# Clustered attention and a rational MLP on one core: a new order of the operations on all five engines

## The chip, the cores and the metric

The kernel runs on one core of one Trainium2 chip. The metric is the device time of one execution in microseconds (us); the time of a kernel is the median of its runs. The trace is that of one profiled execution. Engines are named as in the profile: PE (TensorE), DVE (VectorE), ACT (ScalarE), POOL (GpSimd) and SP (SyncE, which here only issues transfers).

## The reference

Attention in which a query attends to the keys of its own cluster alone, and behind it an MLP whose activation is a quotient of two polynomials:

```python
q_assign = np.argmax(np.einsum('bhsd,hcd->bhsc', q_n, c_n), axis=-1)
k_assign = np.argmax(np.einsum('bhsd,hcd->bhsc', k_n, c_n), axis=-1)
mask = q_assign[:, :, :, None] == k_assign[:, :, None, :]
scores = np.where(mask, scale * np.matmul(q, k.transpose(0, 1, 3, 2)), -1e9)
attn = np.exp(scores - scores.max(-1, keepdims=True))
attn = attn / (attn.sum(-1, keepdims=True) + 1e-9)
x = np.matmul(attn, v).transpose(0, 2, 1, 3).reshape(B * S, H * D)
h = x @ w_in
g = (a[0] + a[1]*h + a[2]*h**2 + a[3]*h**3) / (1 + abs(b[0])*abs(h) + abs(b[1])*h**2 + 1e-6)
out = g @ w_out
```

Here q_n, k_n and c_n are the normalised rows. B = 4, H = 8, S = 768, D = 64, 16 clusters, w_in is 512 x 2048 and w_out 2048 x 512, all in float32.

## The kernel before

Every operand of a matrix product is split into a high and a low float16 half, so that a product is three matmuls. The work goes batch by batch. For each of four pairs of heads `prep` (L944) loads q and k, scales and splits them into `tk` and `tq` (the high half is copied a second time at L1092, and each of the two buffers is transposed by a DMA at L1120), finds the clusters (L1159 to L1208) and splits v into `vhi` and `vlo` (L1249). `attend` (L1256) takes two tiles of 128 queries at a time: scores on PE (`s`, L1278), the maximum on DVE (L1293), the exponential and the high half on ACT (all of ACT's activations stand at the helper's line L551), the low half on DVE (`ah`, L1313), a transpose by DMA (`at<-ah`, L1323), the product with v on PE (`px`, L1332; four groups of 18 matmuls make one `px` bank), the division on DVE (`inv`, `xf`, L1352 to L1358), the split of the result (`xm`, on ACT and on POOL at L1365) and its transpose `x` by DMA (L1372). Batch 0 mostly uses another form, `attend_keys` (L1378). `moe` (L1582) takes 256 tokens and four blocks of 128 columns at a time: `ph` on PE (L1640), |h| and the first step of the cubic on ACT (`u`, `t`), two more steps of it on DVE (`t`, L1661 and L1666, which free the PSUM bank of `ph`), the denominator on POOL (`s`, L1680, L1686, L1703) and ACT, the quotient on DVE (`t`, `s`, L1723, L1733), its low half on POOL (`u`, L1740), and the second product on PE (`po`, L1751), whose sum goes out through `ob`.

A `px` bank and the two `ph` banks come from the same small ring of PSUM banks, so a `px` can start only when the DVE has finished the two `t` operations on an earlier `ph`.

What sets the order: the functions above run no instruction themselves. They hand operations to `Plan` (`op`, L212), with the buffers that each reads and writes, and `Plan.order` (L260) decides in which order they are emitted. It holds the table `ORDER`, five lists, one for each engine, of running numbers of operations. With the table given, each engine takes its operations strictly in the list's order:

```python
turn_of = {e: [self.ops[i] for i in reversed(self.given[e])] for e in engines}
```

An operation still waits, by semaphores, for what it reads and for the buffer that it writes. Within that, `Plan.order` runs a model of the engines that decides in which sequence the five lists are interleaved, and from it which slot of a ring of buffers (eight large buffers, five `ah`, three `at`, two `rv`, two PSUM banks for `ph` and `px`, two for `s`) each tile gets. So a new table moves instructions, the slots of buffers and the places of waits, and nothing else. An engine works strictly in order: an instruction that waits holds up all that stand behind it. The model marks all operations of POOL and some of DVE (`lock=True`: the copies at L1092, the quotient steps at L1723 and L1733) as taking turns at one port.

Of the kernel before, what the change touches and what calls it, by code (L numbers as in the profile page):

```python
# [65 lines left out]
""",  # L66
    "DVE": """
# [103 lines left out]
""",  # L171
}

# [1696 lines left out]
```

## Time and profile before

| what | value |
|---|---|
| three runs | 883.43, 890.54, 881.96 us; median 883.43 us |
| the profiled execution | 889.14 us, its span 887.2 us (1.94 us lie around the span) |
| mean granted PE clock | 0.995 of full speed |
| busy, of the span | PE 94%, DVE 89%, ACT 85%, POOL 65% |
| chain that ended last, by engine | PE 60%, DVE 15%, ACT 11%, DMA 7%, issue 5% |

Busy shares are averages over stages with different limits, so the windows of 40 us and the chain by place say more. The chain is followed back from the last instruction: each piece is what released the next one. On the timelines a bracket at the end of a row gives the engine's idle time just before it and what ended it; POOL's rows often overlap by some hundredths of a microsecond, which means that they ran back to back.

### The profile page before, as it was taken

Reading aid. Unit: us, or ns where it says so; the run is one execution under the profiler, and the core shown is the slowest. Engines: PE = TensorE matmul, PEld = TensorE weight load, DVE = VectorE, ACT = ScalarE, POOL = GpSimd, SP = SyncE. Lnnn points to the kernel's source line nnn. Section 1 sums busy time; section 2 is a strip of 40 time slices with the busy share of each in tenths; the row PEclk is TensorE's granted clock in tenths of the full one; section 3 lists DMA queues with packets and bytes.
Section 4 is the critical chain, followed back from the end, with each engine's and each line's share of the span. In section 5 each row is a group of like instructions: output and inputs, shape, how many; then the busy total and the mean of one; then the engine's idle time right before and its main releaser. Section 6 shows DMA issues by size and latency. Waiting matters only on the chain.

```text
span 887.2 us, 22561 instructions
## 1 busy us (share of the span) xinstructions
PE 835.5 (94%) x8989; PEld 590.7 (67%) x8989; DVE 787.1 (89%) x1396; ACT 757.6 (85%) x1053; POOL 579.0 (65%) x608
## 2 busy tenths in 40 slices
PE   2889998878998999999999999999999999999997
PEld 2557776656676676667676776767677666766763
DVE  6997959999999999999999999999999988767776
ACT  7567799979999899989999999998998888756664
POOL 2264758878777969658778987678767876123221
PEclk9999999999999999999999999999999999999999
DMA  8478688989989699999999999979688887310000
GB/s 289 164 150 197 179 226 212 205 173 160 203 167 207 124 171 199 180 195 211 185 187 165 197 201 165 183 139 186 129 173 138 137 148 116 79 13 24 1 25 24
DMA packets 378025, 138.09 MB, mean 156 GB/s; under 512 B 355776, under 2 KB 372160, under 8 KB 377920
## 3 DMA queue, kind: packets, MB, share of 16 engines
q1 hardware_dynamic: 377920, 136.65, 78.4%
q8 instruction: 70, 1.15, 0.5%
q14 instruction: 35, 0.29, 0.1%
HBM read 41.98 MB, written 6.29 MB: 54 GB/s over the span
## 4 chain that ended last, share of the span: by engine, by line
PE 60%; DVE 15%; ACT 11%; DMA 7%; issue 5%; POOL 1%; SPq 0%; DVEq 0%; ACTq 0%; POOLq 0%
PE ph L1640 19%; PE po L1751 19%; PE px L1332 7%; PE s L1278 7%; DMA at<-ah 4%; ACT s L551 3%; ACT u L551 2%; DVE ah L1313 2%; PE z L1488 2%; DVE s L1293 2%; DMA sq<-tq 2%; DVE top L1436 2%; ACT ah L551 2%; PE px L1507 2%; PE s L1409 1%
## 5 line engine op out<-in xcount | busy, mean ns | idle before, releaser
L1640 PE MATMUL ph<-x,win 128*128 128x256 f16 x2304 | 266.3, 273 | 3.9 <-DVE xf L1358 1.7
L1751 PE MATMUL po<-wout,u 128*128 128x512 f16 x1152 | 268.5, 379 | 0.4 <-DVE u L1740 0.4
L1640 PEld LDWEIGHTS <-win 128*128 128x128 f16 x2304 | 223.9, 98 | 42.9 <-DVE xf L1358 3.5
L1680 POOL TENSOR_TENSOR s<-s,u 128x512 f32<-128x512 f32 x96 | 127.3, 1342 | 119.9 <-ACT s L551 65.3
L1751 PEld LDWEIGHTS <-u 128*128 128x128 f16 x1152 | 110.2, 98 | 115.4 <-DVE u L1740 0.9
L1313 DVE SCALAR_TENSOR_TENSOR ah<-s,ah 128x768 f16<-128x768 f32 x152 | 143.8, 951 | 13.2 <-ACT ah L551 12.6
L551 ACT ACTIVATE s<-s,nm 128x768 f32<-128x768 f32 x152 | 132.4, 874 | 23.1 <-DVE s L1293 18.7
L1293 DVE TENSOR_SCALAR_CACHE_REDUCE s<-s,cc 128x768 f32<-128x768 f32 x144 | 145.2, 1018 | 6.9 <-PE s L1278 6.5
L1278 PE MATMUL s<-sk,sq 128*128 128x384 f16 x608 | 121.1, 326 | 6.6 <-DVE ah L1313 5.4
L551 ACT ACTIVATE ah<-s 128x768 f16<-128x768 f32 x152 | 123.0, 813 | 3.6 <-DMA at<-ah 1.0
L1703 POOL TENSOR_TENSOR s<-s,u 128x512 f32<-128x512 f32 x72 | 111.0, 1553 | 21.3 <-ACT u L551 20.9
L1740 POOL TENSOR_TENSOR u<-s,u 128x512 f16<-128x512 f32 x72 | 85.8, 1200 | 32.1 <-DVE s L1733 17.6
L1332 PEld LDWEIGHTS <-at 128*128 128x128 f16 x2736 | 93.9, 98 | 19.1 <-issue 5.1
L1332 PE MATMUL px<-vhi,at 128*128 128x65 f16 x1824 | 96.7, 195 | 6.2 <-DVE t L1666 3.5
L1332 PE MATMUL px<-vlo,at 128*128 128x64 f16 x912 | 92.5, 193 | 0.0
L1278 PEld LDWEIGHTS <-sq 128*128 128x128 f16 x608 | 55.5, 98 | 45.7 <-DVE ah L1313 8.4
L1661 DVE TENSOR_TENSOR t<-ph,t 128x512 f32<-128x512 f32 x96 | 65.3, 684 | 8.4 <-ACT t L551 8.2
L551 ACT ACTIVATE u<-ph 128x512 f32<-128x512 f32 x96 | 56.8, 596 | 16.5 <-PE ph L1640 16.1
L1733 DVE SCALAR_TENSOR_TENSOR s<-s,t 128x1024 f32<-128x1024 f32 (+1 forms) x49 | 61.5, 1254 | 0.5
L551 ACT ACTIVATE u<-t 128x1024 f16<-128x1024 f32 (+1 forms) x49 | 51.0, 1040 | 11.8 <-DVE t L1723 8.7
L551 ACT ACTIVATE t<-ph,gk 128x512 f32<-128x512 f32 x72 | 55.5, 778 | 0.0
L1723 DVE SCALAR_TENSOR_TENSOR t<-t,gk,u 128x1024 f32<-128x1024 f32 (+1 forms) x37 | 48.4, 1309 | 5.7 <-ACT u L551 5.3
(222 smaller groups left out, 1367.4 us busy)
## 6 DMA issues: line engine op xcount, KB each, us to landing
rwi<-in_moe_w_in_dram SPq DMA_DIRECT2D x16, 512.0 KB, 5.2
rwo<-in_moe_w_out_dram SPq DMA_DIRECT2D x16, 512.0 KB, 5.4
rk<-in_k_dram SPq DMA_DIRECT2D x32, 192.0 KB, 3.0
rq<-in_q_dram SPq DMA_DIRECT2D x32, 192.0 KB, 3.5
rvm<-in_v_dram SPq DMA_DIRECT2D x16, 384.0 KB, 4.6
rv<-in_v_dram SPq DMA_DIRECT2D x16, 384.0 KB, 4.2
out_dram<-ob SPq DMA_DIRECT2D x11, 512.0 KB, 3.8
at<-ah SPq DMA_TRANSPOSE x152, 4.2
```

The source lines that it names most:

```text
L551: lambda: nc.scalar.activation(out=out(), in_=in_(), func=func, **{a: (x() if callable(x) else x) for a, x in kw.items()}),
L1278: nc.tensor.matmul(sc.ap[:, i, :SH], lhsT=st["q" + x].ap[:, j, t, :], rhs=st["k" + x].ap[:, j, ks, :].rearrange("p t c -> p (t c)"), start ...
L1293: lambda nm=nm, view=view: ts(out=view(), in0=view(), scalar1=cc.ap, scalar2=None, op0=ALU.mult, op1=ALU.min, accum_out=nm.ap),
L1313: lambda part=part, view=view: stt(out=part(1), in0=view(), scalar=A_SCALE, in1=part(0), op0=ALU.mult, op1=ALU.subtract),
L1332: nc.tensor.matmul(px.ap[:, i, :w_], lhsT=at.ap[:, p_, kt, :], rhs=vv.ap[:, j, kt, :w_], start=(kt == 0 and vv is vhi and p_ == 0), stop=( ...
L1640: nc.tensor.matmul(ph[i].ap[:, fi * TW : (fi + 1) * TW], lhsT=win[f // 4][:, wpart, c, f % 4 * P : (f % 4 + 1) * P], rhs=xs[c].ap[:, xpart ...
L1661: lambda i=i, th=th, ph=ph: tt(out=th[i].ap, in0=ph[i].ap, in1=th[i].ap, op=ALU.mult),
L1680: lambda i=i, sh=sh, uh=uh: nc.gpsimd.tensor_tensor(out=sh[i].ap, in0=sh[i].ap, in1=uh[i].ap, op=ALU.mult),
L1703: lambda i=i, sh=sh, uh=uh: nc.gpsimd.tensor_tensor(out=sh[i].ap, in0=sh[i].ap, in1=uh[i].ap, op=ALU.mult),
L1733: lambda tw=tw, sw=sw: stt(out=sw(), in0=sw(), scalar=2.0, in1=tw(), op0=ALU.subtract, op1=ALU.mult),
L1740: lambda i=i, sh=sh, gl=gl, g16=g16, e=(nc.vector if gld else nc.gpsimd): e.tensor_tensor(out=gl[i].ap, in0=sh[i].ap, in1=g16()[:, 0, i * ...
L1751: nc.tensor.matmul(po[ti].ap, lhsT=g16()[:, part, c0 : c0 + P], rhs=wout[f // 4][:, wpart, f % 4], start=(k == 0 and f == f_first), stop=( ...
```

## The change

All five lists of `ORDER` are replaced by others. No operation, no buffer, no constant and no line of code is changed. Each list holds the same running numbers as before. Of the operations on PE, 462 of 857 stand at another rank in their list, of those on DVE 751 of 1156, on ACT 591 of 1004, on POOL 455 of 587 and on SP 318 of 394; most by one to five places. One pair of lines of the DVE list as an example (1382 is the copy of keys at L1092, 837 and 838 the two `t` operations at L1661 and L1666, 1265 and 1272 two maxima at L1293):

```diff
-1384 821 1265 817 793 794 795 824 319 320 321 1382 837 838 322 1272 1268 827 828 829 ...
+817 319 793 794 795 824 1265 837 838 320 321 1272 1382 322 1268 827 828 829 ...
```

Three places follow as the engines' instruction streams have them. In a name like `ah_3_5_1_2672` the numbers are the pair of heads, the tile of 128 queries and the head of the pair; in `t_0_0_2699` the block of 256 tokens and the first column block; the last number only tells tiles apart.

First, DVE at about 172 to 178 us of the trace, before:

```order
L1358 TENSOR_TENSOR xf_3_1_2678<-px_3_1_2539,inv_3_1_2669 128x256
L1313 SCALAR_TENSOR_TENSOR ah_3_5_1_2672<-s_3_5_1_2522,ah_3_5_1_2672 128x768
L899 TENSOR_SCALAR g10c_2210<-g10c_2210 128x1
L877 TENSOR_SCALAR g10c_2210<-g10c_2210 128x1
L902 TENSOR_REDUCE g10c_2210<-woe 128x1
L1092 COPY tk_1_2717<-tk_1_2188 128x12x64
L1661 TENSOR_TENSOR t_0_0_2699<-ph_0_0_0_2636,t_0_0_2699 128x512
L1666 SCALAR_TENSOR_TENSOR t_0_0_2699<-t_0_0_2699,gk0c_1244,ph_0_0_0_2636 128x512
L882 TENSOR_TENSOR g10c_2210<-g10c_2210 128x1
L1293 TENSOR_SCALAR s_0_0_1_2725,nm_0_0_1_2755<-s_0_0_1_2725,cc_0_1989 128x2x384
```

And in the changed kernel:

```order
L1358 TENSOR_TENSOR xf_3_1_2672<-px_3_1_2540,inv_3_1_2667 128x256
L1313 SCALAR_TENSOR_TENSOR ah_3_5_1_2669<-s_3_5_1_2581,ah_3_5_1_2669 128x768
L1293 TENSOR_SCALAR s_0_0_0_2525,nm_0_0_0_2692<-s_0_0_0_2525,cc_0_1973 128x2x384
L1661 TENSOR_TENSOR t_0_0_2713<-ph_0_0_0_2634,t_0_0_2713 128x512
L1666 SCALAR_TENSOR_TENSOR t_0_0_2713<-t_0_0_2713,gk0c_1391,ph_0_0_0_2634 128x512
L877 TENSOR_SCALAR g10c_2200<-g10c_2200 128x1
L902 TENSOR_REDUCE g10c_2200<-woe 128x1
L1293 TENSOR_SCALAR s_0_0_1_2720,nm_0_0_1_2754<-s_0_0_1_2720,cc_0_1973 128x2x384
L1092 COPY tk_1_2778<-tk_1_2205 128x12x64
L882 TENSOR_TENSOR g10c_2200<-g10c_2200 128x1
L1313 SCALAR_TENSOR_TENSOR ah_0_0_0_2730<-s_0_0_0_2525,ah_0_0_0_2730 128x768
```

The copy `tk_1` stood ahead of the two `t` operations of the first `ph`; now it stands behind them and behind one more maximum (`s_0_0_1`), and the maximum `s_0_0_0`, which stood ahead of these rows, has come behind `ah_3_5_1`. The small `g10c` operations lie around it in another order.

Second, POOL at about 70 to 77 us, before:

```order
L1194 TENSOR_TENSOR df_2_1025<-df_2_1025,w_90 128x384
L1132 COPY tk_2_719<-mrow 128x12x16
L1133 MEMSET tq_2_975 128x12x16
L1567 TENSOR_TENSOR x_0_0_1099<-rs_0_0_996,x_0_0_1099 128x256
L1208 TENSOR_SCALAR tk_2_719<-df_2_1025 128x12x48
L1208 TENSOR_SCALAR tq_2_975<-df_2_1025 128x12x48
```

And in the changed kernel:

```order
L1132 COPY tk_2_744<-mrow 128x12x16
L1133 MEMSET tq_2_988 128x12x16
L1194 TENSOR_TENSOR df_2_1026<-df_2_1026,w_90 128x384
L1208 TENSOR_SCALAR tk_2_744<-df_2_1026 128x12x48
L1567 TENSOR_TENSOR x_0_0_1098<-rs_0_0_1001,x_0_0_1098 128x256
L1208 TENSOR_SCALAR tq_2_988<-df_2_1026 128x12x48
```

The result of the mask, `tk_2`, is written ahead of `x_0_0` and no longer behind it; `tq_2` stays behind `x_0_0`. SP transposes `tk_2` and then `tq_2`.

Third, DVE at about 453 to 461 us, before:

```order
L1733 SCALAR_TENSOR_TENSOR s_1_0_7139<-s_1_0_7139,t_1_0_7115 128x1024
L1313 SCALAR_TENSOR_TENSOR ah_1_3_0_7321<-s_1_3_0_7255,ah_1_3_0_7321 128x768
L1661 TENSOR_TENSOR t_1_4_7335<-ph_1_4_0_7263,t_1_4_7335 128x512
L1666 SCALAR_TENSOR_TENSOR t_1_4_7335<-t_1_4_7335,gk_3441,ph_1_4_0_7263 128x512
L1293 TENSOR_SCALAR s_1_4_0_7341,nm_1_4_0_7371<-s_1_4_0_7341,cc_1_5819 128x2x384
L1661 TENSOR_TENSOR t_1_4_7335<-ph_1_4_1_7303,t_1_4_7335 128x512
L1666 SCALAR_TENSOR_TENSOR t_1_4_7335<-t_1_4_7335,gk_3441,ph_1_4_1_7303 128x512
L1313 SCALAR_TENSOR_TENSOR ah_1_4_0_7407<-s_1_4_0_7341,ah_1_4_0_7407 128x768
L1293 TENSOR_SCALAR s_1_4_1_7410,nm_1_4_1_7433<-s_1_4_1_7410,cc_1_5819 128x2x384
L1092 COPY tk_3_7437<-tk_3_6772 128x12x64
L1661 TENSOR_TENSOR t_1_8_7431<-ph_1_8_0_7374,t_1_8_7431 128x512
```

And in the changed kernel:

```order
L1733 SCALAR_TENSOR_TENSOR s_1_0_7123<-s_1_0_7123,t_1_0_7103 128x1024
L1661 TENSOR_TENSOR t_1_4_7321<-ph_1_4_0_7264,t_1_4_7321 128x512
L1666 SCALAR_TENSOR_TENSOR t_1_4_7321<-t_1_4_7321,gk_3463,ph_1_4_0_7264 128x512
L1313 SCALAR_TENSOR_TENSOR ah_1_3_0_7337<-s_1_3_0_7255,ah_1_3_0_7337 128x768
L1092 COPY tk_3_7371<-tk_3_6790 128x12x64
L1293 TENSOR_SCALAR s_1_4_0_7345,nm_1_4_0_7376<-s_1_4_0_7345,cc_1_5819 128x2x384
L811 TENSOR_REDUCE vm_7392<-vm_6967 128x1
L1661 TENSOR_TENSOR t_1_4_7321<-ph_1_4_1_7305,t_1_4_7321 128x512
```

The copy `tk_3` has moved up by several places, to directly behind `ah_3_0`. On POOL, what stands around it is the same in both kernels up to the two `xm` at L1365 (two `u`, two `s` of L1680, `s` of L1686, two `xm`); behind these two `xm` the changed list has a `vlo` (L1249), which stood seventeen places later.

Elsewhere on POOL, at about 412 to 416 us, a `vlo` that stood between the two `u` of one block (L1740) now stands five places earlier, ahead of two `s` (L1680), and an `xm` that stood six places later now stands directly ahead of the first of the two `u`. At the end of SP's list one store of the output now stands ahead of the last `x` transpose and no longer behind it.

## Rows read from the trace of the kernel before

**Rows 1.** The page: busy us by engine; POOL at L1680.

```profile
PE 835.5 (94%) x8989; PEld 590.7 (67%) x8989; DVE 787.1 (89%) x1396; ACT 757.6 (85%) x1053; POOL 579.0 (65%) x608
...
L1680 POOL TENSOR_TENSOR s<-s,u 128x512 f32<-128x512 f32 x96 | 127.3, 1342 | 119.9 <-ACT s L551 65.3
```

**Rows 2.** Windows of 40 us: length, busy (instructions), PE clock, DMA share, GB/s.

```profile
160.00:200.00 40.00, 30.01 (x411) 23.88 (x407) 37.88 (x71) 35.28 (x58) 31.47 (x44) 0.96 0.97 180
...
440.00:480.00 40.00, 40.00 (x425) 28.15 (x424) 36.35 (x60) 39.40 (x58) 31.30 (x27) 1.00 0.99 197
```

**Rows 3.** The chain that ended last, 165:186: start, us, what.

```profile
172.25 0.96 DVE ah L1313
...
173.57 3.79 DVE tk L1092
177.36 0.61 DVE t L1661
...
178.89 3.82 PE px L1332 x72
```

**Rows 4.** Timeline of PE, 174 to 180 us.

```profile
174.86 0.81 PE L1278 MATMUL s<-sk,sq 128*128 128x384 f16 x4
178.89 0.22 PE L1332 MATMUL px<-vhi,at 128*128 128x65 f16 x1 [3.22 <-DVE t L1666]
```

**Rows 5.** Timeline of POOL, 172:180: start, us, instruction, idle before.

```profile
173.61 0.68 POOL L1567 TENSOR_TENSOR x<-rs,x 128x256 f16<-128x256 f32 x1
...
177.10 2.62 POOL L1680 TENSOR_TENSOR s<-s,u 128x512 f32<-128x512 f32 x2
179.81 1.05 POOL L1686 TENSOR_SCALAR s<-s 128x1024 f32<-128x1024 f32 x1
```

**Rows 6.** Line L1092: the copies of keys, ns least, median, longest.

```profile
L1092 DVE COPY tk<-tk x12: 348/440/3872, 120.6 to 664.6; 128x768 f16<-128x768 f16 x12
```

**Rows 7.** A window of 2 us in the middle of these `px`.

```profile
180.00:182.00 2.00, 2.00 (x41) 2.00 (x39) 1.54 (x3) 1.20 (x2) 1.99 (x2) 0.50 1.04 318
```

**Rows 8.** The last two `at` transposes: issue in ns, when, landing.

```profile
L1323 SPq DMA_TRANSPOSE at<-ah x2: 1455/1961/2467, 171.7 to 174.2; - x2
...
DMA to landing us min/median/max: 4.0/4.2/4.4
```

**Rows 9.** PE's groups of instructions, 160 to 220.

```profile
L1278 PE MATMUL s<-sk,sq 128*128 128x384 f16 x56 | 11.4, 326 | 4.0 <-DVE ah L1313 4.0
```

**Rows 10.** Timeline of POOL, 66 to 76 us.

```profile
74.24 0.67 POOL L1567 TENSOR_TENSOR x<-rs,x 128x256 f16<-128x256 f32 x1 [3.13 <-ACT x L551]
...
75.53 0.67 POOL L1208 TENSOR_SCALAR tq<-df 128x576 f16<-128x576 f16 x1
```

**Rows 11.** The chain that ended last, 66 to 86 us.

```profile
78.06 5.58 DMA sq<-tq
...
83.69 1.31 PE s L1409 x7
```

**Rows 12.** Timeline of POOL, 405 to 436 us.

```profile
413.13 1.17 POOL L1740 TENSOR_TENSOR u<-s,u 128x512 f16<-128x512 f32 x1
414.25 1.60 POOL L1249 TENSOR_TENSOR vlo<-rv,vhi 128x768 f16<-128x768 f32 x1
```

**Rows 13.** Timeline of PE, 412 to 419 us.

```profile
414.84 1.46 PE L1751 MATMUL po<-wout,u 128*128 128x512 f16 x6
```

**Rows 14.** Timeline of POOL, 452 to 465 us.

```profile
454.17 2.28 POOL L1740 TENSOR_TENSOR u<-s,u 128x512 f16<-128x512 f32 x2 [2.65 <-ACT u L551]
456.91 2.50 POOL L1680 TENSOR_TENSOR s<-s,u 128x512 f32<-128x512 f32 x2 [0.45 <-ACT s L551]
...
460.51 1.30 POOL L1365 TENSOR_TENSOR xm<-xf,xm 128x256 f16<-128x256 f32 x2
463.57 2.32 POOL L1703 TENSOR_TENSOR s<-s,u 128x512 f32<-128x512 f32 x1 [1.76 <-ACT u L551]
```

**Rows 15.** Timeline of DVE, 452 to 465 us.

```profile
455.50 0.75 DVE L1666 SCALAR_TENSOR_TENSOR t<-t,gk,ph 128x512 f32<-128x512 f32 x1
```

258 rows, old and new, of the table ORDER are left out of this document.

## The prediction

> **What bounds the kernel now.** I read the page's busy times first, then the windows of 40 us, then the chain where a window showed idle PE, and last the timelines of what the chain named. PE is the busiest engine, but DVE and ACT are close behind it, so the mean says little [rows 1]. The windows decide: from about 440 us on PE shows 40.00 busy of 40, while DVE has 36.35 and POOL 31.30 [rows 2]. There a better order of DVE, ACT or POOL can give nothing, since PE has no idle time to give back, and a worse one can only add. Between 160 and 200 us it is otherwise: PE is busy for 30.01 of 40, so 10.0 us are idle, and DVE is at 37.88 [rows 2]. That stretch is DVE's, and a gain has to come from there or from ahead of it.
>
> The largest single hole is at 175.7 to 178.9 us. The chain goes through one DVE copy, `tk` at L1092, which holds 3.79 us of it from 173.57 on, then through the `t` operations at L1661 and L1666, and only then `px` begins at 178.89 [rows 3]. PE had finished the scores at 174.86 + 0.81 = 175.67 and then sat idle for 3.22 us, released by that `t` [rows 4]. The copy is a small operation: the median of the twelve is 440 ns, this one took 3872 ns [rows 6]. What stretched it is seen on POOL, which ran back to back from 173.61 to 177.10 (with the instruction under way five in all; those between are of the same kind), and the copy ended as POOL went over to the two `s` at L1680, which wait for ACT [rows 5]. So the copy did not get its turn while POOL had work without a gap. The hole had a second price: after it PE was granted half of its full speed, 0.50 in the window from 180 to 182, that is 1.2 of 2.4 GHz, where the mean of the execution is 0.995 [rows 7]. The 72 matmuls of `px` took 3.82 us there [rows 3]; at the upper level they take half of that at best, 1.9 us.
>
> **The change part by part.** No instruction is added or removed, so every term is a wait that goes, comes or moves. The sum is made against the profiled execution, 889.14 us, which is 0.65% above the median of 883.43 us; I scale at the end.
>
> First term, the copy at 173.6 us. In the changed order both `t` stand ahead of the copy. DVE ends `ah` at 172.25 + 0.96 = 173.2 [rows 3]; then come one maximum (about 1.1 with its accumulator, an estimate from the mean of its kind, 1018 ns on the page), the two `t` (0.61 and about 0.75), done at about 175.7 [rows 3]. That is when PE ends the scores, so the 3.22 us go [rows 4]. What is late next is the last `at`: it is issued at 174.2 and lands 4.0 to 4.4 us later, at about 178.5 [rows 8]. With a last quarter of 18 matmuls (0.44 us at full speed, by 41 in 2.00 us at half speed [rows 7]) `px` ends at about 179.0, and not at 182.7: 3.7 us earlier for PE. But PE does not keep all of it. Between 160 and 220 us the scores wait 4.0 us for DVE's `ah` in smaller pieces [rows 9], so what counts is what DVE gets back. That is 3.79 - 0.44 = 3.35 us, less what the copy waits at its new place. It is reached at about 177.2 (two small `g10c` and one more maximum behind the `t`). POOL then has the two `s` of L1680 and the `s` of L1686, 177.10 to 180.86, back to back [rows 5]. The first of these waits for ACT; over all 96 such operations ACT made POOL idle for 65.3 us, 0.7 us each [rows 1], and here ACT has an exponential to do first that now comes later (its maximum moved behind `ah`). I take it that the copy finds this gap after about 1 us: 3.35 - 1.0 = 2.3 us gained. Bounds: nothing gained if it finds no gap until 180.86, up to 3.2 + 1.9 = 5.1 us if the whole hole and the slow clock behind it go.
>
> On this copy the Trainium skill speaks another language than the row. The row shows the copy waiting while POOL works through five instructions, 3.4 us longer than usual [rows 5, 6]. "SBUF — State Buffer", section "Who interferes with whom", says that VectorE and GpSimd take a shared pair of ports as an exclusive lock for one whole instruction, and that order of issue decides who waits. Read plainly, a waiting copy would lose one POOL instruction, here at most 1.3 us, and the first term would be sure. By the row it can lose a whole chain of them, which is why both ends of the range above are kept. By the rule rival two below would cost 1.3 us at most and no more than the forecast's own range holds; by the row it is a rival.
>
> Second term, POOL at 74 us. Before, `tk` waited behind `x` at L1567, which began at 74.24 after 3.13 us of idle time by ACT [rows 10]. Now `tk` goes first and its transpose can start about 0.7 to 1.3 us earlier; the transpose of `tq` follows it on SP and lands as the chain's next piece, 78.06 + 5.58 = 83.64, right before the scores at 83.69 [rows 11]. `tq` itself is still behind `x`, at 75.53 at the earliest less the 0.65 of `tk` [rows 10], in time for the SP queue. I take -1.0 us, bounds -1.3 and 0 (if DVE is late there instead).
>
> Third term, new waits in the stretch where PE is full. The clearest is at 413 us. The `u` at L1740 that began at 413.13 now has a `vlo` of 1.60 us ahead of it that stood behind it, and an `xm` (0.65, half of 1.30) [rows 12, 14]; ACT makes POOL idle by 0.7 us in the mean ahead of an `s` of L1680 [rows 1], two of which stand in front, and that takes some of it. So this `u` ends about 2.25 - 0.7 = 1.55 us later than 414.30. PE took it for `po` at 414.84, 0.54 us of slack [rows 13]: +1.0 us, bounds 0 and +1.7. The second `u` of that block no longer has the `vlo` between and loses nothing.
>
> All else at nothing. The other ranks move by a few places on engines that wait for PE in the full stretch; what hides them is DVE's 3.65 and POOL's 8.7 us of idle time in each 40 [rows 2]. On SP the last `x` transpose now stands behind a store of the output; the store is ready well before the `ph` that reads this `x`, and a landing takes about 4 us [rows 8]. If that cover is gone, PE waits there for at most a landing, 4 us.
>
> Sum: -2.3 - 1.0 + 1.0 = -2.3 us, 886.8 us against 889.14. Scaled to the median: 883.43 x 886.8 / 889.14 = 881.1 us. By the bounds the sum goes from -5.1 - 1.3 + 0 = -6.4 to 0 + 0 + 1.7 = +1.7 us: 877.1 to 885.1 us is this case's own range.
>
> **The rivals.** A change below 1%, 8.8 us, is about what a measurement of this kernel can't tell from no change: the three runs lie 8.6 us apart.
>
> One: the order does not do what it says. The copy at 177.2 meets POOL's chain again, `xf` behind it is late in place of the `t`, and the gain at 74 us ends in a DVE wait. For it: POOL is back to back there in the rows [rows 5]. Against it: the wait of L1680 on ACT. Time: +1.0 of the third term alone, 884.4 us.
>
> Two, the slower side: the same stall at another place, now where PE is full. The copy `tk_3` is reached at about 456.2, when the `t` that began at 455.50 has ended [rows 15] (`ah` and `t` only change places). POOL's two `u` end at 456.45, and after a gap of 0.45 us two `s` start at 456.91, with `s` and two `xm` behind them until 461.81 [rows 14]. Before, 1.76 us of waiting followed; now a `vlo` of 1.60 fills it [rows 12, 14]. If the copy comes into that gap, it costs nothing. The point from which it turns is some 0.6 us of delay on DVE: then it waits from 456.9 to 461.8, or to 463.4 with the `vlo`, 4.9 to 6.5 us. At 173 us a stall of 3.4 us left PE idle for 3.2 and cost up to 1.9 by the slow clock [rows 3, 4, 7]; by that measure this one costs 4.7 + 1.9 = 6.6 to 6.3 + 1.9 = 8.2 us. With the -2.3 it makes +4.3 to +5.9: 887.7 to 889.3 us; without the gain of the first term up to 891.6.
>
> Three, the faster side: DVE's relief spreads. DVE is what PE waits for in 160 to 200, 10.0 us of idle time [rows 2]; if these small waits go too, since the lists there are reordered throughout, the gain is the 10.0 and the 1.9 of the slow clock with the second term: -12.9, 870.6 us. For it: nearly all of this idle time is named by DVE, ACT or transposes. Against it: DVE is busy for 37.88 of 40, so 2.1 us is all that it can give besides the stall's 3.4; PE can't win more than that for long.
>
> **How the numbers follow.** The forecast has 0.45, rival one 0.22, rival two 0.16, rival three 0.17. Predicted: 881.1 us. The range takes in rival three and most of rival two: 871 to 890 us. Over 1% faster (below 874.6) are rival three and a little of the forecast's lower end: 0.19. Over 1% slower (above 892.3) is rival two without the gain and with the cover on SP gone, or with a second such stall: 0.11. Within 1%: 0.70.
>
> **What would show it.** Right: no `tk` copy of more than 2 us near 177 us; PE's idle time ahead of that `px` below 1 us and no granted clock below 0.9 in 176 to 184; PE busy by 2 to 4 us more in the window 160 to 200; the scores that started at 83.69 start near 82.5; the `po` near 414 waits for `u` by about 1 us. Wrong: a copy at L1092 of several microseconds anywhere after 240 us; PE windows below 39 of 40 between 440 and 680 us; a `ph` near the end that waits for `x`.

## The result and the profile after

The changed kernel takes 878.67 us (median of 12 runs, 875.33 to 881.35); the kernel before, run on the same chip, takes 884.14 us (12 runs, 881.96 to 890.54). The ratio is 0.992, 95% interval 0.9894 to 0.9947: 7.1 us less by the ratio, with 4.7 and 9.4 us as its ends, 5.5 us by the medians. That is faster by 0.8%; the interval reaches 1.1%. The profiled execution took 880.69 us with a span of 878.9 us, 8.3 us less than the span of the one before. One profile is one execution: ten of the profiles below come from kernels with exactly the old lists up to about 170 us, and they reach the first `ph` anywhere between 166.73 and 169.59 us (169.03 in the one before). So differences of profiles are taken from place to place, and not from the start.

The page of the changed kernel, busy us by engine, then POOL at L1680 (to set beside [rows 1]):

```profile
PE 833.7 (95%) x8989; PEld 590.4 (67%) x8989; DVE 774.9 (88%) x1396; ACT 756.4 (86%) x1053; POOL 572.0 (65%) x608
...
L1680 POOL TENSOR_TENSOR s<-s,u 128x512 f32<-128x512 f32 x96 | 123.4, 1304 | 119.3 <-ACT s L551 66.6
```

The counts are the same, and yet DVE was busy for 12.2 us less and POOL for 7.0 us less; ACT changed by 1.2 us. The copies at L1092 alone make 5.6 us of it (16.0 before, 10.4 after). That fewer operations of DVE and POOL met at the shared port would explain the rest too, but no run shows it for them.

Windows of the changed kernel, columns as in [rows 2]:

```profile
160.00:200.00 40.00, 34.35 (x398) 25.99 (x397) 37.64 (x79) 39.94 (x64) 36.55 (x44) 0.91 0.94 177
...
440.00:480.00 40.00, 40.00 (x441) 29.20 (x438) 37.15 (x64) 37.47 (x56) 33.21 (x33) 1.00 1.03 198
```

Between 160 and 200 us PE is busy for 4.34 us more than before, and the later window is as full as it was [rows 2].

The first place, in the timelines of DVE, then PE, then POOL of the changed kernel:

```profile
172.62 0.69 DVE L1661 TENSOR_TENSOR t<-ph,t 128x512 f32<-128x512 f32 x1 [0.64 <-ACT t L551]
173.35 0.75 DVE L1666 SCALAR_TENSOR_TENSOR t<-t,gk0c,ph 128x512 f32<-128x512 f32 x1
...
175.07 0.48 DVE L1092 COPY tk<-tk 128x768 f16<-128x768 f16 x1
```

```profile
174.25 0.19 PE L1332 MATMUL px<-vhi,at 128*128 128x65 f16 x1 [0.52 <-DVE g10c L902]
```

```profile
173.06 2.27 POOL L785 TENSOR_TENSOR wout<-wwo,wout 128x512 f16<-128x512 f32 x2
175.77 2.50 POOL L1680 TENSOR_TENSOR s<-s,u 128x512 f32<-128x512 f32 x2 [0.44 <-ACT s L551]
```

Both `t` stand ahead of the copy, `px` waits for 0.52 us where it waited for 3.22 [rows 4], and the copy takes 0.48 us where it took 3.87 [rows 6]. It came at 175.07, POOL's `wout` ended at 175.33, and the next POOL instruction was 0.44 us late by ACT: the gap ahead of L1680 on which the forecast counted was there.

The copies at L1092 over the whole kernel (ns least, median, longest), against [rows 6]:

```profile
L1092 DVE COPY tk<-tk x12: 332/355/566, 123.9 to 663.7; 128x768 f16<-128x768 f16 x12
```

Half speed did not go away, it moved. A window of 2 us of the changed kernel, then the rows of PE's timeline ahead of it:

```profile
192.00:194.00 2.00, 2.00 (x12) 1.39 (x10) 2.00 (x5) 2.00 (x4) 2.00 (x3) 0.50 0.45 86
```

```profile
185.38 0.18 PE L496 MATMUL vb<-column,ones 128*128 128x1 bf16 x1 [0.66 <-DVE t L1666]
186.25 0.81 PE L1278 MATMUL s<-sk,sq 128*128 128x384 f16 x4 [0.69 <-DVE ah L1313]
...
189.49 1.44 PE L1278 MATMUL s<-sk,sq 128*128 128x384 f16 x4 [1.24 <-DVE ah L1313]
```

The granted clock fell during the third of these waits (1.00 up to 188.4 us, 0.50 from 188.6) and stayed at 0.50, that is 1.2 of 2.4 GHz, through 194; before, it fell at the end of one wait of 3.22 us [rows 4, 7]. The mean clock of 160 to 200 is 0.91, lower than before (0.96 [rows 2]), so part of the 4.34 us is only work that lasts longer. By the starts of the same `ph`, PE was 1.35 us ahead of the profile before at the first (169.03 there) and 5.62 us ahead at the one at 199.25: 4.3 us won all the same.

The second place is seen in PE's timeline:

```profile
82.33 0.82 PE L1409 MATMUL s<-sk,sq 128*128 128x384 f16 x4
82.99 0.82 PE L1488 MATMUL z<-sq,sk 128*128 128x256 f16 x6
83.64 1.46 PE L1409 MATMUL s<-sk,sq 128*128 128x384 f16 x8
```

The scores begin at 82.33 and no wait for `sq` stands between them; before, they went on only at 83.69, when `sq` had landed [rows 11].

At the third place, `po` follows its neighbours without a gap in the changed kernel, and the wait comes one operation later. PE's timeline, then the chain:

```profile
415.27 1.46 PE L1751 MATMUL po<-wout,u 128*128 128x512 f16 x6
...
419.22 0.20 PE L1332 MATMUL px<-vhi,at 128*128 128x65 f16 x1 [1.39 <-DMA at<-ah]
```

```profile
412.44 0.97 DVE s L1293
413.42 5.76 DMA at<-ah
...
419.22 0.72 PE px L1332 x18
```

This `px` waits 1.39 us for a transpose that took 5.76 us. Nothing like it stands in the kernel before at that place. The late operand is `at`, not `u`.

### The profile page after: what moved, and what is told of

It is laid out like the page before. It is cut to its first block, busy times and chain, and to the rows that moved or that the text cites. A ratio compares the mean times of both kernels' runs of the same rounds, so it can differ in the third digit from the quotient of the medians.

```text
span 878.9 us, 22609 instructions
## 1 busy us (share of the span) xinstructions
PE 833.7 (95%) x8989; PEld 590.4 (67%) x8989; DVE 774.9 (88%) x1396; ACT 756.4 (86%) x1053; POOL 572.0 (65%) x608
## 3 DMA queue, kind: packets, MB, share of 16 engines
q8 instruction: 70, 1.15, 0.6%
## 4 chain that ended last, share of the span: by engine, by line
PE 60%; DVE 11%; ACT 11%; DMA 9%; issue 4%; SPq 3%; POOL 1%; DVEq 0%; ACTq 0%; POOLq 0%
PE po L1751 20%; PE ph L1640 19%; PE s L1278 6%; PE px L1332 6%; DMA at<-ah 4%; ACT s L551 3%; PE px L1507 2%; DVE s L1293 2%; PE z L1488 2%; ACT ah L551 2%; DVE ah L1313 2%; DMA rwi<-in_moe_w_in_dram 2%; ACT u L551 2%; SPq L1323 2%; DMA sq<-tq 1%
## 5 line engine op out<-in xcount | busy, mean ns | idle before, releaser
L1680 POOL TENSOR_TENSOR s<-s,u 128x512 f32<-128x512 f32 x96 | 123.4, 1304 | 119.3 <-ACT s L551 66.6
L1293 DVE TENSOR_SCALAR_CACHE_REDUCE s<-s,cc 128x768 f32<-128x768 f32 x144 | 145.3, 1019 | 9.4 <-PE s L1278 8.6
L1703 POOL TENSOR_TENSOR s<-s,u 128x512 f32<-128x512 f32 x72 | 111.9, 1568 | 23.0 <-ACT u L551 22.6
L1740 POOL TENSOR_TENSOR u<-s,u 128x512 f16<-128x512 f32 x72 | 83.7, 1172 | 38.9 <-DVE s L1733 20.7
L1661 DVE TENSOR_TENSOR t<-ph,t 128x512 f32<-128x512 f32 x96 | 65.6, 685 | 13.3 <-ACT t L551 13.0
L1723 DVE SCALAR_TENSOR_TENSOR t<-t,gk,u 128x1024 f32<-128x1024 f32 (+1 forms) x37 | 50.5, 1365 | 10.8 <-ACT u L551 10.6
```

What stands on the lines that cost most here:

```text
L1293: lambda nm=nm, view=view: ts(out=view(), in0=view(), scalar1=cc.ap, scalar2=None, op0=ALU.mult, op1=ALU.min, accum_out=nm.ap),
L1661: lambda i=i, th=th, ph=ph: tt(out=th[i].ap, in0=ph[i].ap, in1=th[i].ap, op=ALU.mult),
L1680: lambda i=i, sh=sh, uh=uh: nc.gpsimd.tensor_tensor(out=sh[i].ap, in0=sh[i].ap, in1=uh[i].ap, op=ALU.mult),
L1703: lambda i=i, sh=sh, uh=uh: nc.gpsimd.tensor_tensor(out=sh[i].ap, in0=sh[i].ap, in1=uh[i].ap, op=ALU.mult),
L1740: lambda i=i, sh=sh, gl=gl, g16=g16, e=(nc.vector if gld else nc.gpsimd): e.tensor_tensor(out=gl[i].ap, in0=sh[i].ap, in1=g16()[:, 0, i * ...
```

## The experiments

Each kernel was run in five rounds beside the kernel before (6 to 12 runs each), whose median was 885.74 to 886.13 us. In the diffs, numbers are the running numbers of the table; `H` stands for all operations emitted ahead of the `ph` that starts at 234 us in the trace before, `W` for those from there to the `ph` at 298 us. Prices in us are the ratio less one, times 885.

**The pair of `t` first, nothing else.** Kernel before, list of DVE:

```diff
-... 319 320 321 1382 837 838 322 1272 ...
+... 319 320 321 837 838 1382 322 1272 ...
```

> The kernel before, with one edit: on DVE the two t operations (L1661, L1666) stand directly ahead of the tk copy that took 3.87 us, all else in the old order. Theory (the hole at 175.7 us is made by the copy holding up these two, and PE keeps what it gets back, as it did in the changed kernel, where the lead grew by 4.0 us at this px): the px starts at about 176, PE's idle time ahead of it falls from 3.22 to below 1 us and no slow clock follows; 3 to 4.5 us faster than before. Rival (DVE gives back at once what PE gains, since it is busy for 37.9 of 40 us there and the copy itself still waits): the px starts early, but the time falls by 0 to 1 us only.

Measured: 0.998 (0.9964 to 0.9996), -1.8 us, between the two expectations. DVE's timeline of this kernel:

```profile
172.84 0.75 DVE L1666 SCALAR_TENSOR_TENSOR t<-t,gk0c,ph 128x512 f32<-128x512 f32 x1
173.50 1.78 DVE L1092 COPY tk<-tk 128x768 f16<-128x768 f16 x1
175.20 1.22 DVE L882 TENSOR_TENSOR g10c<-g10c 128x1 f32<-128x1 f32 x1
```

The copy still waited, now behind the `t`, and a small operation of one column behind it took 1.22 us. In PE's timeline `px` started early but stood still once more, for the last `at`, and half speed came later here too (0.50 from 192 to 194 us):

```profile
176.76 0.20 PE L1332 MATMUL px<-vhi,at 128*128 128x65 f16 x1 [1.01 <-DMA at<-ah]
```

This one exchange is worth a gain, a quarter of the whole by its middle value (its interval is 0.4 to 3.2 us).

**The copy back at its old place in the new order.** Kernel after, list of DVE: 1382 directly behind 1265, ahead of both `t`.

```diff
-... 1265 837 838 320 321 1272 1382 322 ...
+... 1265 1382 837 838 320 321 1272 322 ...
```

> The changed kernel, with one edit: the tk copy is put back ahead of the two t operations, directly behind the maximum that now stands there. Theory (order alone decides, as the copy meets POOL's unbroken run from its old place): the copy again takes more than 2 us and px begins 2 to 4 us later than 174.25; 2 to 5 us slower than the changed kernel, so 2 to 5 us faster than before. Rival (POOL's new order leaves gaps there): the copy takes 0.4 to 1.2 us at this place too, and the time stays that of the changed kernel within 1 us, some 6 us faster than before.

Measured: 0.9924 (0.9897 to 0.9952), the same as the changed kernel. The copy in DVE's timeline and the instruction of POOL that was under way:

```profile
173.49 0.83 DVE L1092 COPY tk<-tk 128x768 f16<-128x768 f16 x1
```

```profile
173.43 0.69 POOL L778 TENSOR_SCALAR wwo<-wwo,wos 128x512 f32<-128x512 f32 x1
```

At the old place the copy took 0.83 us and not 3.87. POOL has no gap here either, from 171.65 to 177.08, but its new list has a short scaling of weights (`wwo`, L778) at this point, and the copy came in behind it. So DVE's list alone does not explain the first place: in this profile of POOL's new order the copy was cheap at the old place too, and the time of seven runs agrees.

**New lists up to 234 us, old ones behind, and the reverse.** Each of the five lists is put together as follows (in the tail about a dozen operations lie on the other side of the cut):

```diff
+head: [i for i in after[e] if i in H] + [i for i in before[e] if i not in H]
+tail: [i for i in before[e] if i in H] + [i for i in after[e] if i not in H]
```

> The changed order for all operations that the old order emits ahead of the ph at about 234 us, the old order for all behind it. The profiles of before and after differ by 6.5 us at that place and by 8.3 us at the end. Theory (the gain is made by the waits in the first 240 us, and the full stretch of PE behind them only carries it): 5 to 7 us faster than before. Rival (the later lists make it, the lead at 234 us would have been lost under the old ones): 0 to 3 us faster.

> The counterpart: the old order up to about the ph at 234 us, the changed order behind it. Theory: 0 to 3 us faster than before (waits of 1.01 and 1.25 us near 282 to 287 us go, 1.39 near 418 and 0.89 near 522 us come). Rival: 4 us or more faster.

Measured: head 0.9957 (0.994 to 0.9974), -3.8 us; tail 0.9956 (0.9937 to 0.9976), -3.9 us. The two add to -7.7 us against -7.1 of the whole. Half of the gain is made behind 234 us, where the forecast expected none. By the starts of the same `ph`, against the profile before, the tail was 2.01 us ahead at 234 and 4.35 at 298: 2.3 us won. (The 2.7 us in a later expectation count from a `ph` at 278 us that stands at another rank in the new list of PE.) The head was 6.67 us ahead at 234 and only 3.20 at 298: under the old lists behind the cut it lost half of its lead again.

**The copy in a form of another kind.** Kernel before; this one copy is a multiplication by 1.0 that also writes a minimum nobody reads:

```diff
-nc.vector.tensor_copy(out=cols(nm + "2", 0), in_=cols(nm + "1", hi))
+ts(out=cols(nm + "2", 0), in0=cols(nm + "1", hi), scalar1=1.0, scalar2=None, op0=ALU.mult, op1=ALU.min, accum_out=acc.ap)
```

> The kernel before in its old order; only the one tk copy that took 3.87 us is made by another form of DVE instruction, a multiplication by one that also writes out the minimum (the form of L1293, which took 1.01 to 1.03 us wherever it stood). Theory (the fast copy takes turns with POOL at a port, the other form does not): it takes 1.0 us at the same place, the px behind it starts 2.5 to 3 us earlier, and the time falls as in the run with the two t ahead of the copy, by 1 to 3 us. Rival (whatever is issued on DVE there waits, for a semaphore or its data): it takes 3 us or more and the time stays that of before.

Measured: 0.9988 (0.997 to 1.0006), -1.1 us, not told from nothing. Line L1092 in DVE's timeline of this kernel:

```profile
171.36 0.94 DVE L1092 TENSOR_SCALAR_CACHE_REDUCE tk<-tk 128x768 f16<-128x768 f16 x1
```

At the same place, beside the same POOL instructions, it took 0.94 us. It began 0.05 us behind the start of POOL's `x`; where the plain copy began there it took 1.93 to 1.96 us, and where it began 0.12 us ahead 3.85 to 3.87 (three and four profiles, below). So the wait belongs to the fast form of the copy and not to its operands, and the fair comparison in this one profile is with 1.9 us.

**All five new lists, but only from 234 to 298 us.**

```diff
+[i for i in before[e] if i in H] + [i for i in after[e] if i in W] + [i for i in before[e] if i not in H and i not in W]
```

> The kernel before, with the changed order on all five engines only for the operations that the old order emits between the ph at 234 us and the ph at 298 us. In the run with the changed order behind 234 us the profile gained 2.7 us between 278 and 298 us and then moved up and down with no net gain. Theory (the second half of the gain is made at 280 to 287 us, where three DVE operations in a row took 2.13, 1.92 and 1.42 us and not 1.1, 1.28 and 0.35, with POOL's u and s beside them): 2 to 4 us faster than before. Rival (the second half comes in many small pieces behind 298 us): 0 to 1 us faster.

Measured: 0.9957 (0.9936 to 0.9978), -3.8 us, all that the tail gives. PE's windows, the kernel before and then this kernel:

```profile
280.00:300.00 20.00, 17.74 (x236) 12.69 (x233) 19.37 (x33) 16.69 (x25) 15.73 (x14) 1.00 0.82 159
```

```profile
280.00:300.00 20.00, 20.00 (x237) 14.61 (x235) 18.37 (x31) 19.55 (x29) 18.46 (x17) 1.00 1.01 187
```

PE was idle for 2.26 us in these 20 us of the kernel before; here it has no idle time left. In the kernel before these are two waits in PE's timeline:

```profile
283.06 2.79 PE L1640 MATMUL ph<-x,win 128*128 128x256 f16 x24 [1.01 <-DVE xf L1358]
287.10 0.81 PE L1278 MATMUL s<-sk,sq 128*128 128x384 f16 x4 [1.25 <-DVE ah L1313]
```

They are no accident of one profile: the four profiles with all five old lists there have both (1.00 to 1.04 and 1.24 to 1.25 us), the six with all five new lists have neither. Three of the six have a wait for an `at` there instead, of 0.84 to 1.70 us.

**POOL's instructions near 280 us moved, nothing else.** Kernel before, list of POOL:

```diff
-... 1364 1210 1005 1030 1212 1004 1029 ...
+... 1210 1005 1029 1212 1004 1030 1364 ...
```

> The kernel before with one edit on POOL alone, at 277 to 286 us: the xm that ran at 277.16 comes behind the s and u, and the two s of L1703 change places, as in the changed order; DVE, ACT, PE and SP keep the old lists. Theory (POOL's order alone decides what the three DVE operations lose at the port): they take below 1.5 us each, PE's waits of 1.01 and 1.25 us there shrink to below 0.6 us, 1.5 to 3 us faster than before. Rival (the old lists of the other engines bring the same meeting about, or the two s merely wait at another place): 0 to 1 us faster.

Measured: 1.0013 (0.9989 to 1.0037), no difference. Two of DVE's three operations there were stretched as before, the first one less; these are the timelines of DVE, of the kernel before and then of this one:

```profile
280.06 2.13 DVE L1072 SCALAR_TENSOR_TENSOR tq<-rq,qsc,tq 128x768 f16<-128x768 f32 x1
...
282.92 1.92 DVE L1723 SCALAR_TENSOR_TENSOR t<-t,gk0c,u 128x1024 f32<-128x1024 f32 x1
284.76 1.42 DVE L1092 COPY tq<-tq 128x768 f16<-128x768 f16 x1
```

```profile
278.23 1.55 DVE L1072 SCALAR_TENSOR_TENSOR tq<-rq,qsc,tq 128x768 f16<-128x768 f32 x1
280.51 1.92 DVE L1723 SCALAR_TENSOR_TENSOR t<-t,gk0c,u 128x1024 f32<-128x1024 f32 x1
282.35 1.43 DVE L1092 COPY tq<-tq 128x768 f16<-128x768 f16 x1
```

In the changed kernel the same three take 1.11, 1.28 and 0.33 us. Moving POOL's side by hand did not part them. PE's first wait fell to 0.43 us, the second stayed at 1.25, and a new one for an `at` took back more than was won:

```profile
292.12 0.20 PE L1332 MATMUL px<-vhi,at 128*128 128x65 f16 x1 [1.72 <-DMA at<-ah]
```

**Two more moves in the new order.** Kernel after: one quotient step on DVE behind an `ah` that PE waits for near 188 us, one load on SP behind an `at` transpose.

```diff
-DVE: 855 at its place
+DVE: ... 1289 855 ...
-SP: 1644 at its place
+SP: ... 1488 1644 ...
```

> The changed kernel with two more moves: on DVE the s of L1733 at 186.16 us comes behind the ah for which the scores wait from 188.25 to 189.49 us, and on SP the rv load at 272.76 us comes behind two at transposes, for the last of which px waits 1.70 us near 281 us. Theory: PE's wait before those scores falls to below 0.3 us and the half-speed stretch from 188 to 195 us does not come; 2 to 4 us faster than the changed kernel, 9 to 11 us faster than before. Rival (the stretches behind are bound by DVE and ACT and take it back): the changed kernel's time within 1 us.

Measured: 0.9936 (0.9916 to 0.9955), no better than the changed kernel's 0.992. In the trace the wait for `at` near 283 us, 1.70 us in the changed kernel, is gone, but the wait for `ah` is hardly shorter (1.15 us for 1.24), one of 1.54 us for another DVE operation follows it, and half speed comes there as before.

**Both gains in one kernel.** The lists of the window from 234 to 298 us and the exchange of the first experiment:

```diff
+five lists: after[e] for i in W
-DVE: ... 1382 837 838 ...
+DVE: ... 837 838 1382 ...
```

> The kernel before with two edits at once: the copy tk_1 behind the two t operations (alone: -1.8 us) and the changed lists for the operations between the ph at 234 and the ph at 298 us (alone: -3.8 us). Theory (two holes 60 us apart that PE waits through one after the other, so their prices add): -5 to -6 us, ratio 0.993 to 0.995. Rival (DVE or a transfer gives the first gain back before the second place is reached, or both relieve the same queue): no better than the second alone, ratio 0.9955 to 0.997.

Measured: 0.9945 (0.9925 to 0.9965), -4.9 us, at the edge of what the theory gave. The parts alone make -5.6. The prices add within what can be told; that they give something back is not excluded. The copy behind the `t`, 1.78 us in the profile of the exchange alone, took 0.55 us here under the same lists.

**The window with the new lists of some engines only.**

```diff
+c2: after[e] in W for DVE, POOL; before[e] for ACT, PE, SP
+c3: after[e] in W for ACT, PE, SP; before[e] for DVE, POOL
+c4: after[e] in W for ACT, DVE, PE, SP; before[e] for POOL
```

> The kernel before with the changed lists of DVE and POOL alone for the operations between the ph at 234 and the ph at 298 us; ACT, PE and SP keep the order of before. Theory (in that stretch it is the meeting of DVE's and POOL's operations at the shared port that was changed): nearly all of the -3.8 us of the five lists together, ratio 0.9955 to 0.997, and DVE's tq at L1072, t at L1723 and the tq copy near 276 us at about 1.1, 1.3 and 0.4 us. Rival (it is the order in which ACT and SP give out work, the port only follows): within 1 us of the kernel before, ratio 0.999 to 1.001.

> The complement of the run with DVE and POOL: the changed lists of ACT, PE and SP alone for the operations between the ph at 234 and the ph at 298 us. Theory (the port order decides): within 1 us of the kernel before, ratio 0.999 to 1.001, with the DVE operations near 280 us still at 1.4 to 2.1 us. Rival (ACT and SP decide): -2.5 to -3.8 us, ratio 0.9955 to 0.997.

> The changed lists of ACT, DVE, PE and SP for the operations between the ph at 234 and the ph at 298 us, POOL's list as before. Theory (DVE's own order decides which of its operations meet POOL's, POOL's rank changes are secondary, as the run that moved POOL's operations near 280 us alone gave nothing): -2.5 to -3.8 us, ratio 0.9955 to 0.997. Rival (POOL's order is needed too): less than 1.5 us, ratio above 0.998.

Measured: DVE and POOL alone 1.0065 (1.0041 to 1.009), +5.8 us; ACT, PE and SP alone 0.9977 (0.9959 to 0.9994), -2.0 us; all but POOL 1.006 (1.0036 to 1.0084), +5.3 us. No theory named a loss. Where it comes from is in the traces. With POOL's old list, DVE's timeline has this:

```profile
276.13 0.17 DVE L893 RECIPROCAL g<-g 128x2 f32<-128x2 f32 x1 [8.69 <-POOL g L861]
276.21 1.27 DVE L1723 SCALAR_TENSOR_TENSOR t<-t,gk0c,u 128x1024 f32<-128x1024 f32 x1
```

and PE's this:

```profile
278.40 2.72 PE L1278 MATMUL s<-sk,sq 128*128 128x384 f16 x8 [6.36 <-DVE ah L1313]
```

The new list of DVE has the reciprocal `g` several places earlier. That is free if POOL's `g` (L861) comes early too, as it does in POOL's new list; in the old one it stands behind two `s`, another `s` and an `xm`, DVE stands still for 8.69 us, and PE waits 6.36 us for the `ah` behind it. With DVE and POOL alone, the chain of the trace runs through SP:

```profile
284.76 1.19 SPq L1372
...
286.63 4.84 DMA at<-ah
...
291.52 0.73 PE px L1332 x18
```

There `px` waited 2.75 us for an `at` whose transpose SP issued only behind the transpose of an `x` at L1372; another `px` had waited 1.29 us for an `at` at 277.86 us. Two of the three DVE operations near 280 us were short in this run (1.01 and 0.33 us at L1072 and L1092; 2.36 at L1723), and it lost all the same. And with ACT, PE and SP alone the two operations at L1072 and L1092 were as long as before or nearly so (1.93 and 1.43 us), and still 2.0 us were won.

## Why the prediction was right, and where its sum was not

The forecast, faster within 1%, came true: 878.67 us against 881.1, inside the forecast's own range of 877.1 to 885.1. The sum of -2.3 us was too small; 4.7 to 9.4 were measured. That the number came as near as 2.4 us is in part luck: its second and third terms cancelled and neither came as described, and half of the gain was made where the sum had nothing.

**The first term** (-2.3, bounds 0 and -5.1). Its mechanism held: the `t` ahead of the copy, a gap of POOL ahead of L1680, no `tk` copy above 0.57 us. The 1.0 us set aside for the copy at its new place was not needed (0.48 us against a median of 0.36), and the late `at` did not come in the changed kernel: there `ah` goes ahead of the maximum that the sum put behind it without moving `ah` up. In the exchange alone, where that maximum stays, it came, 1.01 us. These are the first and the fifth `ph` (groups of 12 matmuls) in PE's timeline of the kernel before and of the changed one:

```profile
169.03 2.78 PE L1640 MATMUL ph<-x,win 128*128 128x256 f16 x24
...
183.62 1.48 PE L1640 MATMUL ph<-x,win 128*128 128x256 f16 x12 [0.28 <-DVE xf L1358]
```

```profile
167.67 5.40 PE L1640 MATMUL ph<-x,win 128*128 128x256 f16 x48
...
177.55 1.48 PE L1640 MATMUL ph<-x,win 128*128 128x256 f16 x12 [0.20 <-DVE xf L1358]
```

PE won 4.7 us between them, and in the profile of the exchange 2.5; the exchange was measured at 1.8. What the order alone can't tell is that the wait has two outcomes. Seven profiled kernels have exactly the old lists up to 234 us: the kernel before, the tail (but for a few operations at the cut), POOL at 280, the window, and the three with some engines only. In four the copy took 3.85 to 3.87 us, in three 1.93 to 1.96 us, and in these three PE had gained 3.2 us on the other four by the fifth `ph`. Line L1092 of one of the second kind, the window from 234 to 298 us:

```profile
L1092 DVE COPY tk<-tk x12: 335/380/1934, 120.1 to 657.6; 128x768 f16<-128x768 f16 x12
```

In the long ones the copy began 0.11 to 0.12 us ahead of POOL's `x`, in the short ones 0.05 to 0.07 us behind its start. So a difference of under 0.2 us in step between the two engines went with 3.2 us. The window 160 to 200 of the three short ones has a mean clock of 1.00, where [rows 2] has 0.96: the half speed of [rows 7] did not follow a copy of 1.9 us. The profile before was a long one and its median a mixture: three of seven times 3.2 us, 1.4, is what a typical run has already. By this estimate from few profiles the exchange is worth 2.5 - 1.4 = 1.1 us (0.4 to 3.2 measured) and the changed kernel's first place 3.3. It is a rough one: the copy in the other form won 4.2 us at this place in its profile and should be worth 2.8, and -0.5 to 2.7 were measured. The term was sized from one of two outcomes; that its -2.3 lies between 1.1 and 3.3 is luck.

**The second term** (-1.0). It is not shown. The scores start 0.64 us earlier (82.33 for 82.97), but PE was 0.56 us ahead 16 us earlier already; the same row of PE's timeline in the changed kernel and in the kernel before:

```profile
66.66 2.79 PE L1488 MATMUL z<-sq,sk 128*128 128x256 f16 x24
```

```profile
67.22 2.79 PE L1488 MATMUL z<-sq,sk 128*128 128x256 f16 x24
```

What is left is the wait of 0.38 us for `sq`, and it too is one of two outcomes: of the ten profiles with the old lists there, four have it (0.26 to 0.38 us) and six have not, like that of the exchange at 172 us:

```profile
80.73 1.47 PE L1409 MATMUL s<-sk,sq 128*128 128x384 f16 x8
```

The four profiles with the new lists there don't have it. So this term is worth some 0.1 us in the mean, an estimate from these profiles. The new lists up to 234 us give -3.8 us; beside the -1.8 of the exchange about 2 us of it have no place.

**The third term** (+1.0). A wait of 1.39 us came at 417.8 us, of the size foretold, but for `at` and not for `u`, so the mechanism was wrong.

**"All else at nothing", and "a gain has to come from there or from ahead of it".** This is the step that failed. It rested on the windows from 440 us on, and nothing had been said of 240 to 440: PE is idle there for 2.26 us between 280 and 300 alone. The lists for that stretch by themselves gave -3.8 us, as much as all that was foreseen and more. (The windows from 440 us on are not all full either: in the kernel before PE has 39.23 and 39.57 of 40 between 680 and 760 us.)

**Why that stretch gains** is settled only in part. The two waits of 1.0 and 1.25 us go with the old lists and come back with them. To be rid of them the lists have to agree with each other: two parts of them lose 5 to 6 us by waits from engine to engine that the new lists had moved on both sides at once. The nearer story, that DVE's operations stretched by POOL held PE, is not shown: moving POOL's away left two of three stretched, with ACT, PE and SP alone 2.0 us were won while two of the three were as long as before or nearly so, and with DVE and POOL alone two of the three were short and 5.8 us were lost. How the -3.8 us divides between the port and the hand-overs stays open.

**The rivals.** That the order doesn't do what it says fell with the copy of 0.48 us. The stall of `tk_3` did not come: that copy took 0.48 us as well, in DVE's timeline of the changed kernel

```profile
448.87 0.48 DVE L1092 COPY tk<-tk 128x768 f16<-128x768 f16 x1
```

The chances did not fit this rival's own price: at 887.7 to 891.6 us it lies below the limit of 892.3, and yet 0.11 of its 0.16 was put above it, for further losses that had no chance of their own. The third rival, all small waits of 160 to 200 gone, did not come either: PE still lacks 5.65 of 40 us there, 1.24 of them in one wait for `ah` at 188 us with half speed behind it. The gain near 280 us is not its relief spreading: the lists of that stretch make it by themselves.

## What to carry to other kernels

Price an order of operations stretch by stretch and with the lists of all engines together: a part of the lists under the others' old ones is another program, and here two such parts lost 5 us and more where the whole won 4. Before saying where a gain can't come from, read the windows of the whole span. And a stall that depends on how two engines happen to be in step is one draw in each profile; before it is priced, several profiles of the same order should show whether it has one length or two. Both waits that the forecast read from its one profile, for the copy and for `sq`, were of this kind, and the two near 280 us that it passed over stood in all four profiles of the old lists there.

## What the runs showed that was not expected

A copy of 768 columns of float16 on DVE, 0.35 us when nothing is beside it, waited through five POOL instructions in a row in four profiles, and through two in three, under the same order. The same data in the form that writes out an accumulator took 0.94 us at that place. The Trainium skill, "SBUF — State Buffer", section "Who interferes with whom", says that the form with an accumulator does not take the shared ports, and this trace agrees: 0.94 us where the plain copy in the same step took 1.93 to 1.96. The Trainium skill says there, too, that who issues first has the pair for its whole instruction. Everywhere else in the fourteen profiles the copies came in behind the one POOL instruction that was under way, as in the changed kernel at 175.07 us, but not in these seven and in the first experiment. Why a copy that is ready is passed over there and not elsewhere, no run tells.
